# Grouped-query softmax attention: K in 8 KB pieces with two heads on alternate partitions, V in two transfers a pair

## The chip, the cores and the metric

The kernel runs on one core of one Trainium2 chip. The metric is the device time of one execution in microseconds (us). The times of before are the median of three runs; the profile is of one further execution.

## What is computed

There are 16 batches, 32 query heads and 8 key/value heads, so four query heads share one K and one V. Each query head has 16 rows, each K and V has 2048 keys, and the head dimension is 128. All arrays are bf16.

```python
def reference(q, k, v):
    B, Hq, Sq, D = q.shape            # 16, 32, 16, 128
    Hkv = k.shape[1]                  # 8; k, v are (16, 8, 2048, 128)
    k = jnp.repeat(k, Hq // Hkv, axis=1)
    v = jnp.repeat(v, Hq // Hkv, axis=1)
    scores = jnp.einsum("bhqd,bhkd->bhqk", q, k) * D ** -0.5
    p = _softmax(scores, axis=-1)
    return jnp.einsum("bhqk,bhkd->bhqd", p, v)
```

## The kernel before

The 128 combinations of batch and K/V head are worked off in NP = 64 pairs. The 4 x 16 query rows of one K/V head fill 64 rows, so a pair fills the 128 partitions: head g of the pair has rows 64g to 64g+63. K and V of one pair are 1 MB each; a chunk of Q holds the rows of eight pairs (256 KB).

Per pair p the work goes through these steps.

- SyncE (the SP queue) issues every transfer, in a written-out order: K of pair t, then V of pair t-3 (`VLAG`), then the store of pair t-7 (`SLAG`), with a chunk of Q now and then. It waits when a buffer is not free: six K buffers `Kn` (freed by the transposes, L142), eight V buffers `Vb` (freed by the PV matmuls, L152). In `Kn`, a partition holds 16 successive keys (4 KB) of head 0 and 16 of head 1; `Vb` is laid out in the same way.
- VectorE transposes K in 32 x 32 blocks of four bytes, one instruction for each head (`kt`, L254 to L264), into one of three `KT` buffers.
- TensorE multiplies: 32 matmuls of 512 columns into the single `S_ps` (L217). They read `KT` as bf16 with every second element skipped.
- VectorE multiplies the scores by minus the scale, writes them to `Sneg` in f32 and keeps each row's minimum, which is minus the maximum (L277).
- ScalarE writes the exponentials to `P` in bf16, with the sum of each row (L306). It reads `Sneg` in another order than it is stored in, and so sets the order of the keys in `P`.
- TensorE transposes `P` in eight blocks, two bf16 as one f32 (L232), ScalarE copies them to `PT` (L316), TensorE multiplies with V (L243, 32 matmuls), and ScalarE scales the result by the reciprocal of the sum (L326). SyncE stores it (L166).

TensorE and ScalarE follow the lists `pe_prog` and `act_prog`, VectorE the loop at L273. S of pair p+1 is put ahead of the transposes and PV of pair p. The transposes of K for pair p+2 come behind the minimum of pair p. So the loads run some pairs ahead of the arithmetic.

Of the kernel before, what the change touches and what calls it, by code (L numbers as in the profile page):

```python
# [5 lines left out]
ACT = mybir.ActivationFunctionType  # L6
ALU = mybir.AluOpType
BF16 = mybir.dt.bfloat16
# [15 lines left out]
def bass_standalone__gqa_softmax__sampling_kernel(  # L24
# [21 lines left out]
    iota_t = sb("iota_t", [128, 128], I32)  # L46
    ident = sb("ident", [128, 128], BF16)
    ident4 = sb("ident4", [128, 128], F32)
    Kn = [sb(f"Kn{i}", [128, 2, J * 128], BF16) for i in range(NK)]
    Vb = [sb(f"Vb{i}", [128, 2, J, 128], BF16) for i in range(NV)]  # L50

    KT = [sb(f"KT{i}", [128, 2, J * 64], F32) for i in range(NKT)]
    Qn = [sb(f"Qn{i}", [128, 8, 128], BF16) for i in range(NQ)]

    QT = [sb(f"QT{i}", [128, 4, 1024], BF16) for i in range(2)]
# [27 lines left out]

    qf = q.rearrange("b h s d -> (b h s) d")
    of = out.rearrange("b h s d -> (b h s) d")
    kf = k.rearrange("b h s d -> (b h) (s d)").rearrange("g (a x) -> a g x", a=128)
    vf = v.rearrange("b h s d -> (b h) (s d)").rearrange("g (a x) -> a g x", a=128)


    pe_prog, act_prog = [], []
# [35 lines left out]
    with nc.Block() as block:  # L128
# [8 lines left out]
        @block.sync  # L137
        def _(sp):
            def load_k(p):
                s = p % NK  # L140
                if p >= NK:
                    sp.wait_ge(sem_kt, 2 * (p - NK) + 2)  # L142
                if p == 0:
                    for g in range(2):
                        sp.dma_start(Kn[s][:, g, :], kf[:, g, :]).then_inc(sem_k0[g], 16)  # L145
                else:
                    sp.dma_start(Kn[s][:, :, :], kf[:, 2 * p:2 * p + 2, :]).then_inc(sem_k[s], 16)

            def load_v(p):
                s = p % NV  # L150
                if p >= NV:
                    sp.wait_ge(sem_pv, p - NV + 1)  # L152
                dst = Vb[s][:, :, :, :].rearrange("a g j d -> a g (j d)")
                sp.dma_start(dst, vf[:, 2 * p:2 * p + 2, :]).then_inc(sem_v[s], 16)

            def load_q(c):
                s = c % NQ
                if c >= NQ:
                    sp.wait_ge(sem_st, last_q[c - NQ, 3] + 1)
                src = qf[1024 * c:1024 * (c + 1), :].rearrange("(a j) d -> a j d", j=8)  # L160
                sp.dma_start(Qn[s][:, :, :], src).then_inc(sem_q[s], 16)

            def store(p):
                s = p % NO
                sp.wait_ge(sem_nm, p + 1)
                sp.dma_start(of[128 * p:128 * (p + 1), :], Osb[s][:, :]).then_inc(sem_o[s], 16)  # L166

            for t in range(NP + SLAG + 1):
                if t < NP:
                    load_k(t)  # L170
                for c in range(NQC):
                    if t == max(0, 8 * c - QLEAD):
                        load_q(c)
                if 0 <= t - VLAG < NP:
                    load_v(t - VLAG)
                if 0 <= t - SLAG < NP:
                    store(t - SLAG)
            for s in range(NO):
                sp.wait_ge(sem_o[s], 16 * (NP // NO))

        @block.tensor
        def _(pe):
            pe.wait_ge(sem_id, 3)

            def free(u):
                if u >= NSTAGE:
                    pe.wait_ge(sem_ev, u - NSTAGE + 1)

            for op in pe_prog:
                if op[0] == "QT":  # L190
                    _, c, i, u = op
                    if i == 0:
                        pe.wait_ge(sem_q[c % NQ], 16 * (c // NQ + 1))
                    free(u)
                    dst = stage_ap(u).bitcast(BF16)
                    src = Qn[c % NQ][:, :, :].rearrange("p j (b c e) -> p j b e c", b=2, e=2)
                    b, e = divmod(i, 2)
                    for j in range(8):
                        for r in range(4):
                            ins = pe.transpose(dst[32 * r:32 * (r + 1), 128 * j:128 * (j + 1)], src[:, j, b, e, :], ident[:, :])  # L200
                    ins.then_inc(sem_st, 1)
                elif op[0] == "S":
                    _, p = op
                    pe.wait_ge(sem_kt, 2 * p + 2)
                    if p >= 1:
                        pe.wait_ge(sem_max, p)
                    c, i = divmod(p, 8)
                    if i == 0:
                        pe.wait_ge(sem_ev, last_q[c, 3] + 1)
                    kt = KT[p % NKT][:, :, :].bitcast(BF16).rearrange("p g (t b x e) -> p g b e t x", t=J // 2, b=2, e=2)  # L210
                    qt = QT[c % 2]
                    for acc in range(4):
                        b, e = divmod(acc, 2)
                        for r in range(4):
                            rows = slice(32 * r, 32 * (r + 1))
                            for g in range(2):
                                ins = pe.matmul(  # L217
                                    S_ps[64 * g:64 * (g + 1), 512 * r:512 * (r + 1)],
                                    qt[rows, acc, 128 * i + 64 * g:128 * i + 64 * (g + 1)],
                                    kt[rows, g, b, e, :, :],  # L220
                                    start=(acc == 0), stop=(acc == 3),
                                )
                    ins.then_inc(sem_s, 1)
                elif op[0] == "PT":
                    _, p, h, u = op
                    if h == 0:
                        pe.wait_ge(sem_exp, p + 1)
                    free(u)
                    dst = stage_ap(u)
                    for t in range(4):  # L230
                        x = 4 * h + t
                        ins = pe.transpose(dst[:, 128 * t:128 * (t + 1)], P[p % 2][:, 128 * x:128 * (x + 1)], ident4[:, :])  # L232
                    ins.then_inc(sem_st, 1)
                elif op[0] == "PV":
                    _, p = op
                    pe.wait_ge(sem_ev, last_p[p, 1] + 1)
                    pe.wait_ge(sem_v[p % NV], 16 * (p // NV + 1))
                    if p >= 1:
                        pe.wait_ge(sem_nm, p)
                    pt = PT[p % NPT][:, :, :].bitcast(BF16).rearrange("p t (q e) -> p t e q", e=2)  # L240
                    for j in range(J):
                        for g in range(2):
                            ins = pe.matmul(  # L243
                                O_ps[64 * g:64 * (g + 1), 0:128],
                                pt[:, j // 2, j % 2, 64 * g:64 * (g + 1)],
                                Vb[p % NV][:, g, j, :],
                                start=(j == 0), stop=(j == J - 1),
                                skip_group_check=True,
                            )
                    ins.then_inc(sem_pv, 1)  # L250

        @block.vector
        def _(dve):
            def kt(p, g):  # L254
                if p == 0:
                    dve.wait_ge(sem_k0[g], 16)
                else:
                    dve.wait_ge(sem_k[p % NK], 16 * (p // NK + (1 if p % NK else 0)))
                if p >= NKT:
                    dve.wait_ge(sem_s, p - NKT + 1)  # L260
                dve.transpose(  # L261
                    KT[p % NKT][:, g, :].rearrange("p (t b a e) -> p t e b a", t=J // 2, b=2, e=2),
                    Kn[p % NK][:, g, :].bitcast(F32).rearrange("p (t e b c) -> p t e b c", e=2, b=2, c=32),
                ).then_inc(sem_kt, 1)  # L264

            def recip(p):
# [1 line left out]
                dve.reciprocal(rrec[:, p:p + 1], rowsum[:, p:p + 1]).then_inc(sem_rec, 1)  # L268

            for p in range(2):  # L270
                for g in range(2):
                    kt(p, g)
            for p in range(NP):  # L273
                dve.wait_ge(sem_s, p + 1)
                if p >= 2:
                    dve.wait_ge(sem_exp, p - 1)  # L276
                dve.tensor_scalar(  # L277
                    Sneg[p % 2][:, :], S_ps[:, :], -scale, None,
                    op0=ALU.mult, op1=ALU.min, accum_out=nbias[:, p:p + 1],
                ).then_inc(sem_max, 1)  # L280
                if p >= 1:
                    recip(p - 1)
                if p + 2 < NP:
                    for g in range(2):
                        kt(p + 2, g)
            recip(NP - 1)

        @block.scalar
        def _(act):
            for op in act_prog:  # L290
# [9 lines left out]
                elif op[0] == "exp":  # L300
                    _, p = op
                    act.wait_ge(sem_max, p + 1)
                    if p >= 2:
                        act.wait_ge(sem_st, last_p[p - 2, 1] + 1)

                    act.activation(  # L306
                        P[p % 2][:, :].bitcast(BF16).rearrange("p (t r x) -> p t r x", t=8, r=4),
                        Sneg[p % 2][:, :].rearrange("p (r t x) -> p t r x", t=8, r=4), ACT.Exp,
                        bias=nbias[:, p:p + 1], scale=-1.0, accum_out=rowsum[:, p:p + 1],
                    ).then_inc(sem_exp, 1)  # L310
                elif op[0] == "pe":
# [44 lines left out]
```

## Time and profile before

| what | value |
|---|---|
| median of 3 runs (lowest, highest) | 358.48 us (357.37, 358.52) |
| profiled execution | 359.66 us; span of its instructions 357.7 us |
| granted TensorE clock | 0.924 |
| busy share PE, DVE, ACT | 69%, 83%, 70% |
| bytes moved by DMA, mean rate | 139.22 MB, 389 GB/s |
| instructions | 12753 |

The busy shares are of the span. An engine counts as busy while one of its instructions runs. The DMA rows give the mean over the 16 DMA engines of the core. A packet is one piece of a transfer that one DMA engine moves; the increment of a semaphore that ends each engine's part of a transfer is a packet of 4 bytes.

### The profile page before, as it was taken

To read this page: it belongs to the slowest core of one execution; us is meant where nothing else is said; L and a number is where in the kernel's file an instruction comes from. 1 tells how busy PE (TensorE), PEld (TensorE's weight loads), DVE (VectorE), ACT (ScalarE), POOL (GpSimd) and SP (SyncE) were. 2 spreads that over 40 slices of the span, in tenths; PEclk is the share of its full clock that TensorE was granted. 3 is DMA by queue.
4 is the path that set the end of the run, shared out by engine and by line. 5 is a ranking of instruction groups with operands and counts; after the bars stand their busy time and mean duration, and the time that the engine had idled before them with its cause. 6 is when DMAs were issued, how large, how long until landed. Compare 5 with 4: busy or idle time off the path is not lost.

```text
span 357.7 us, 12753 instructions
## 1 busy us (share of the span) xinstructions
PE 248.2 (69%) x5632; PEld 171.7 (48%) x5632; DVE 296.1 (83%) x320; ACT 249.4 (70%) x353; POOL 1.4 (0%) x7
## 2 busy tenths in 40 slices
PE   2587786686776587776677775776766777667675
PEld 2355554454444364454444554454544555444444
DVE  2879979979699839998798699699778889996880
ACT  3469867778478568788676588478676688765674
POOL 1000000000000000000000000000000000000000
PEclk9769989999899969999998899899889899998898
DMA  7999999999999999999999999999999999999930
GB/s 292 414 408 408 410 407 408 411 412 412 410 412 409 410 412 407 412 413 408 409 411 412 411 407 410 411 411 413 409 409 412 401 409 410 410 411 404 377 139 7
DMA packets 45253, 139.22 MB, mean 389 GB/s; under 512 B 11408, under 2 KB 11408, under 8 KB 45200
## 3 DMA queue, kind: packets, MB, share of 16 engines
q1 hardware_dynamic: 45200, 138.42, 97.4%
q8 instruction: 44, 0.72, 0.8%
q14 instruction: 9, 0.07, 0.1%
HBM read 136.31 MB, written 2.10 MB: 387 GB/s over the span
## 4 chain that ended last, share of the span: by engine, by line
PE 51%; issue 26%; ACT 17%; DVE 3%; DMA 1%; SPq 0%; DVEq 0%; ACTq 0%
PE O_ps L243 20%; PE S_ps L217 18%; ACT PT L316 14%; PE ST_ps L232 8%; PE ST_ps L200 5%; DVE KT L261 2%; ACT QT L296 2%; DMA Qn<-in_q_dram 1%; ACT P L306 1%; DVE Sneg L277 1%; SPq L145 0%; ACT O L326 0%; DVE rrec L268 0%; DVEq L276 0%; ACTq L315 0%
## 5 line engine op out<-in xcount | busy, mean ns | idle before, releaser
L277 DVE TENSOR_SCALAR_CACHE_REDUCE Sneg<-S_ps 128x2048 f32<-128x2048 f32 x64 | 146.1, 2283 | 46.1 <-PE S_ps L217 45.7
L261 DVE STREAM_TRANSPOSE KT<-Kn 128x1024 f32<-128x1024 f32 x128 | 150.7, 1216 | 6.9 <-DMA Kn<-in_k_dram 6.9
L306 ACT ACTIVATE P<-Sneg,nbias 128x2048 bf16<-128x2048 f32 x64 | 128.4, 2006 | 24.1 <-DVE Sneg L277 24.1
L243 PE MATMUL O_ps<-Vb,PT 128*64 128x128 bf16 x2048 | 76.3, 230 | 84.3 <-ACT PT L316 55.4
L243 PEld LDWEIGHTS O_ps<-Vb,PT 128*64 128x64 bf16 x2048 | 65.6, 116 | 100.3 <-ACT PT L316 68.0
L316 ACT ACTIVATE PT<-ST_ps 128x512 f32<-128x512 f32 x128 | 70.1, 596 | 38.8 <-PE ST_ps L232 38.8
L217 PE MATMUL S_ps<-KT,QT 32*64 32x512 bf16 x2048 | 82.5, 432 | 6.1 <-DVE Sneg L277 2.5
L232 PE MATMUL ST_ps<-ident,P 128*128 128x128 f32 x512 | 76.3, 296 | 6.5 <-ACT P L306 6.2
L232 PEld LDWEIGHTS ST_ps<-ident,P 128*128 128x128 f32 x512 | 60.4, 151 | 28.7 <-ACT P L306 18.0
L296 ACT ACTIVATE QT<-ST_ps 128x1024 bf16<-128x1024 bf16 x32 | 32.4, 1023 | 36.0 <-PE ST_ps L200 35.8
L217 PEld LDWEIGHTS S_ps<-KT,QT 32*64 32x64 bf16 x2048 | 28.5, 110 | 30.3 <-issue 13.4
L200 PE MATMUL ST_ps<-ident,Qn 128*32 128x128 bf16 x1024 | 22.9, 239 | 10.0 <-DMA Qn<-in_q_dram 6.4
L200 PEld LDWEIGHTS ST_ps<-ident,Qn 128*32 128x32 bf16 x1024 | 17.2, 106 | 23.9 <-issue 23.8
L326 ACT ACTIVATE O<-O_ps,rrec 128x128 bf16<-128x128 f32 x64 | 23.0, 360 | 6.4 <-PE O_ps L243 6.2
L306 ACT ACTIVATION_READ_ACCUMULATOR P<-Sneg,nbias 128x1 f32 x64 | 12.5, 195 | 0.0
L268 DVE RECIPROCAL rrec<-rowsum 128x1 f32<-128x1 f32 x64 | 10.1, 158 | 2.1 <-ACT P L306 2.1
L277 DVE DVE_READ_ACCUMULATOR Sneg<-S_ps 128x1 f32 x64 | 5.3, 82 | 0.0
L296 ACT ACT_TABLE_LOAD x1 | 1.3, 1283 | 0.7 <-PEq L341 0.7
L134 POOL TENSOR_SCALAR ident<-iota_t 128x128 bf16<-128x128 int32 x1 | 0.5, 534 | 0.1
L135 POOL TENSOR_SCALAR ident<-iota_t 128x128 f32<-128x128 int32 x1 | 0.5, 526 | 0.0
L132 POOL IOTA iota_t<- 128x128 int32 x1 | 0.2, 234 | 0.4 <-POOLq L341 0.4
L341 POOL MEMSET const-bfloat16-1.0<- 128x1 bf16 x1 | 0.1, 101 | 0.0
(3 smaller groups left out, 0.3 us busy)
## 6 DMA issues: line engine op xcount, KB each, us to landing
Vb<-in_v_dram SPq DMA_DIRECT2D x64, 1024.0 KB, 16.0
Kn<-in_k_dram SPq DMA_DIRECT2D x63, 1024.0 KB, 15.0
Qn<-in_q_dram SPq DMA_DIRECT2D x8, 256.0 KB, 14.3
out_dram<-O SPq DMA_DIRECT2D x64, 32.0 KB, 13.9
Kn<-in_k_dram SPq DMA_DIRECT2D x2, 512.0 KB, 3.9
```

The costliest lines, as they stand in the source:

```text
L134: gp.tensor_scalar(ident[:, :], iota_t[:, :], 0.0, None, op0=ALU.is_equal).then_inc(sem_id, 1)
L200: ins = pe.transpose(dst[32 * r:32 * (r + 1), 128 * j:128 * (j + 1)], src[:, j, b, e, :], ident[:, :])
L217: ins = pe.matmul(S_ps[64 * g:64 * (g + 1), 512 * r:512 * (r + 1)], qt[rows, acc, 128 * i + 64 * g:128 * i + 64 * (g + 1)], kt[rows, g, b, ...
L232: ins = pe.transpose(dst[:, 128 * t:128 * (t + 1)], P[p % 2][:, 128 * x:128 * (x + 1)], ident4[:, :])
L243: ins = pe.matmul(O_ps[64 * g:64 * (g + 1), 0:128], pt[:, j // 2, j % 2, 64 * g:64 * (g + 1)], Vb[p % NV][:, g, j, :], start=(j == 0), sto ...
L261: dve.transpose(KT[p % NKT][:, g, :].rearrange("p (t b a e) -> p t e b a", t=J // 2, b=2, e=2), Kn[p % NK][:, g, :].bitcast(F32).rearrange ...
L268: dve.reciprocal(rrec[:, p:p + 1], rowsum[:, p:p + 1]).then_inc(sem_rec, 1)
L277: dve.tensor_scalar(Sneg[p % 2][:, :], S_ps[:, :], -scale, None, op0=ALU.mult, op1=ALU.min, accum_out=nbias[:, p:p + 1],).then_inc(sem_max, 1)
L296: act.activation(QT[c % 2][:, i, :].rearrange("p (a j) -> p a j", j=8), stage_ap(u).bitcast(BF16).rearrange("p (j a) -> p a j", j=8), ACT. ...
L306: act.activation(P[p % 2][:, :].bitcast(BF16).rearrange("p (t r x) -> p t r x", t=8, r=4), Sneg[p % 2][:, :].rearrange("p (r t x) -> p t r ...
L316: act.activation(PT[p % NPT][:, 4 * h:4 * (h + 1), :].rearrange("p t q -> p (t q)"), stage_ap(u), ACT.Copy,).then_inc(sem_ev, 1)
L326: act.activation(Osb[p % NO][:, :], O_ps[:, 0:128], ACT.Copy, scale=rrec[:, p:p + 1]).then_inc(sem_nm, 1)
```

## The change

K of a pair is loaded with 32 successive keys (8 KB) of one head in each partition; even partitions belong to head 0 and odd ones to head 1. Each of the two transposes now takes one half of every partition's bytes, 16 keys of both heads, where it took one head before. `KT` gets another layout: the matmul for head g reads pairs of bf16 elements that stand 4 bytes apart, and successive pairs stand 16 bytes apart. The instruction of the minimum writes `Sneg` in a permuted order, in runs of 32 elements, and the exponential reads it in runs of 128 where it read runs of 64. The keys in `PT` are then in an order for which V needs keys of even 4 KB pieces in partitions 0 to 63 and those of odd pieces in 64 to 127. V of a pair is therefore loaded by two transfers of 512 KB to 64 partitions each, and the PV matmuls wait for both. Engine by engine, the sequence of instructions is the same but for SyncE's, which has 64 transfers more (265 instead of 201).

```diff
-    Kn = [sb(f"Kn{i}", [128, 2, J * 128], BF16) for i in range(NK)]
+    Kn = [sb(f"Kn{i}", [128, 2 * J * 128], BF16) for i in range(NK)]
-    KT = [sb(f"KT{i}", [128, 2, J * 64], F32) for i in range(NKT)]
+    KT = [sb(f"KT{i}", [128, 2 * J * 64], F32) for i in range(NKT)]
...
-    kf = k.rearrange("b h s d -> (b h) (s d)").rearrange("g (a x) -> a g x", a=128)
-    vf = v.rearrange("b h s d -> (b h) (s d)").rearrange("g (a x) -> a g x", a=128)
+    kf = k.rearrange("b h s d -> (b h s d)").rearrange("(p g a x) -> p a g x", p=NP, g=2, a=64)
+    vf = v.rearrange("b h s d -> (b h) (s d)").rearrange("g (a h x) -> h a g x", a=64, h=2)
...
                 if p == 0:
-                    for g in range(2):
-                        sp.dma_start(Kn[s][:, g, :], kf[:, g, :]).then_inc(sem_k0[g], 16)
+                    for h in range(2):
+                        x = slice(2048 * h, 2048 * (h + 1))
+                        sp.dma_start(Kn[s][:, x], kf[p, :, :, x]).then_inc(sem_k0[h], 16)
                 else:
-                    sp.dma_start(Kn[s][:, :, :], kf[:, 2 * p:2 * p + 2, :]).then_inc(sem_k[s], 16)
+                    sp.dma_start(Kn[s][:, :], kf[p, :, :, :]).then_inc(sem_k[s], 16)
...
-                sp.dma_start(dst, vf[:, 2 * p:2 * p + 2, :]).then_inc(sem_v[s], 16)
+                for h in range(2):
+                    sp.dma_start(dst[64 * h:64 * (h + 1), :, :], vf[h, :, 2 * p:2 * p + 2, :]).then_inc(sem_v[s], 16)
...
-                    kt = KT[p % NKT][:, :, :].bitcast(BF16).rearrange("p g (t b x e) -> p g b e t x", t=J // 2, b=2, e=2)
+                    kt = KT[p % NKT][:, :].bitcast(BF16).rearrange("p (b m a g x e) -> p g b e m a x", b=2, m=J, a=16, g=2, x=2, e=2)
...
-                    pe.wait_ge(sem_v[p % NV], 16 * (p // NV + 1))
+                    pe.wait_ge(sem_v[p % NV], 32 * (p // NV + 1))
...
                 dve.transpose(
-                    KT[p % NKT][:, g, :].rearrange("p (t b a e) -> p t e b a", t=J // 2, b=2, e=2),
-                    Kn[p % NK][:, g, :].bitcast(F32).rearrange("p (t e b c) -> p t e b c", e=2, b=2, c=32),
+                    KT[p % NKT][:, :].rearrange("p (b h t x e) -> p h t e b x", b=2, h=2, t=J // 2, e=2)[:, h, :, :, :, :],
+                    Kn[p % NK][:, 2048 * h:2048 * (h + 1)].bitcast(F32).rearrange("p (t e b c) -> p t e b c", e=2, b=2, c=32),
...
                 dve.tensor_scalar(
-                    Sneg[p % 2][:, :], S_ps[:, :], -scale, None,
+                    Sneg[p % 2][:, :].rearrange("p (m r x) -> p r m x", r=4, x=32),
+                    S_ps[:, :].rearrange("p (r m x) -> p r m x", r=4, x=32), -scale, None,
...
-                        P[p % 2][:, :].bitcast(BF16).rearrange("p (t r x) -> p t r x", t=8, r=4),
-                        Sneg[p % 2][:, :].rearrange("p (r t x) -> p t r x", t=8, r=4), ACT.Exp,
+                        P[p % 2][:, :].bitcast(BF16).rearrange("p (t h x) -> p t h x", t=8, h=2),
+                        Sneg[p % 2][:, :].rearrange("p (h t x) -> p t h x", t=8, h=2), ACT.Exp,
```

More of the change, by code (lines that the diff above doesn't have):

```diff
@@ L219, in _ @@
                                     qt[rows, acc, 128 * i + 64 * g:128 * i + 64 * (g + 1)],
-                                    kt[rows, g, b, e, :, :],
+                                    kt[rows, g, b, e, :, :, :],
                                     start=(acc == 0), stop=(acc == 3),
@@ L253, in _, with kt @@
         def _(dve):
-            def kt(p, g):
+            def kt(p, h):
                 if p == 0:
-                    dve.wait_ge(sem_k0[g], 16)
+                    dve.wait_ge(sem_k0[h], 16)
                 else:
@@ L270, in _ @@
             for p in range(2):
-                for g in range(2):
-                    kt(p, g)
+                for h in range(2):
+                    kt(p, h)
             for p in range(NP):
@@ L283, in _ @@
                 if p + 2 < NP:
-                    for g in range(2):
-                        kt(p + 2, g)
+                    for h in range(2):
+                        kt(p + 2, h)
             recip(NP - 1)
```

## The prediction

> **What bounds the kernel now.** I first read the page's slices of the span and its DMA queues.
>
> ```profile
> DVE  2879979979699839998798699699778889996880
> DMA  7999999999999999999999999999999999999930
> GB/s 292 414 408 408 410 407 408 411 412 412 410 412 409 410 412 407 412 413 408 409 411 412 411 407 410 411 411 413 409 409 412 401 409 410 410 411 404 377 139 7
> q1 hardware_dynamic: 45200, 138.42, 97.4%
> ```
>
> The compute engines' digits go up and down; the DMA digit is 9 from the second slice to the 38th, and the rate stays at 401 to 414 GB/s up to the 37th. A rate that does not move while its consumers do is a limit of its own. The table by stages says it again: 409 GB/s from 18 to 340 us, at a share over 1, because records of neighbouring packets overlap a little.
>
> ```profile
> 0.00:17.90 17.90, 7.46 (x196) 5.34 (x197) 10.17 (x9) 7.15 (x7) 1.45 (x7) 0.87 0.91 353
> 17.90:340.00 322.10, 230.13 (x5234) 158.54 (x5234) 278.47 (x301) 231.50 (x330) 0.00 (x0) 0.93 1.03 409
> 340.00:357.70 17.70, 10.60 (x212) 7.79 (x206) 7.41 (x12) 10.78 (x16) 0.00 (x0) 0.90 0.20 71
> ```
>
> Then I sorted the trace's records of the packets on that queue by size. The median packet takes 159 ns for 4096 bytes, 84 ns for 2048, 18 ns for 256 and 9 ns for the 4 bytes of a semaphore. That is a straight line: 9 ns for each packet and 0.0366 ns for each byte (27.3 bytes per ns and engine). A pair costs each of the 16 engines 16 packets of K and 16 of V (32 x 159 = 5.09 us), 8 of the store (0.14), three increments (0.03) and an eighth of a Q chunk (0.09): 5.34 us, times 64 = 342 us. All records of the queue add up to 5573.7 us over 16 engines, 348.4 us each; the difference is a small number of long packets. The span is 357.7 us.
>
> Next, the costliest groups and the waits, for how much room the rest has.
>
> ```profile
> L277 DVE TENSOR_SCALAR_CACHE_REDUCE Sneg<-S_ps 128x2048 f32<-128x2048 f32 x64 | 146.1, 2283 | 46.1 <-PE S_ps L217 45.7
> L261 DVE STREAM_TRANSPOSE KT<-Kn 128x1024 f32<-128x1024 f32 x128 | 150.7, 1216 | 6.9 <-DMA Kn<-in_k_dram 6.9
> L306 ACT ACTIVATE P<-Sneg,nbias 128x2048 bf16<-128x2048 f32 x64 | 128.4, 2006 | 24.1 <-DVE Sneg L277 24.1
> L217 PE MATMUL S_ps<-KT,QT 32*64 32x512 bf16 x2048 | 82.5, 432 | 6.1 <-DVE Sneg L277 2.5
> ```
>
> VectorE is the busiest. Where it runs closed up, the timeline has the minimum at 151.04 and again at 155.57 us: 4.53 us a pair, against 5.34 of DMA. So there is 0.8 us a pair of cover over VectorE. The chain that ended last is 51% TensorE and 26% "issue" and names DMA for 1% only; I read it behind the rate, because the arithmetic's loops wait on each other and hide that buffers arrive late. SyncE's waits (next fence) show buffers that are not yet free; its issues, 0.42 us at the start, have a median of 1.2 us (K) and 2.2 us (V) later, so the queue itself is also full.
>
> ```profile
> SPq L154 <- PE O_ps L243: 66.0, 36, 3.9
> SPq L166 <- ACT O L326: 43.0, 36, 5.6
> SPq L147 <- DVE KT L261: 17.1, 11, 4.0
> ```
>
> **K in 8 KB pieces.** For 63 pairs, 16 packets of 4 KB per engine become 8 of 8 KB. By the line an 8 KB packet takes 9 + 300 = 309 ns; the trace has packets of 8192 bytes on the queue that loads instructions (q14), the shortest at 307 to 309 ns. Two old packets take 318, so 8 x 9 = 72 ns a pair are saved: 63 x 0.072 = -4.5 us. The bounds are 0 (the piece is cut at 4 KB again) and -4.5. I take -4.5, since the 8192-byte records are there. Pair 0 keeps two transfers of 4 KB pieces: 0.
>
> **V in two transfers, the issue.** Each of the 64 added transfers brings one increment per engine, 64 x 9 ns = +0.6 us. On SyncE the added issue costs 0.42 us, the smallest of L154; queued behind it are the store and the next K. 64 x 0.42 = 27 us are covered by the 126 us of waits above. Without that cover it would be 27 us at most. I take 0. The PV matmuls wait for the later half, where they waited for the whole; V comes ahead of use by the depth of eight buffers: 0.
>
> **V in two transfers, the transport.** This is the term that decides, and the trace has no row for it: every transfer of before spans 128 partitions. The lower bound is that a packet to one of 64 partitions still takes 159 ns: 0. The upper bound is that a transfer to half of the partitions takes as long as one to all: 16 x 159 = 2.54 us more per pair, 64 x 2.54 = +163 us. Between them lies the case in which the 16 engines, served by half as many doors to the partitions, move their payload back to back on eight: 256 packets over eight at 150 ns (the line's 300 ns for 8 KB, halved) are 4.80 us instead of 2.54, so +2.26 a pair, +144 us. I take this, near the upper end, as a judgement: the rate of the line is the same for loads and stores and for all sizes, which speaks for a fixed width on the way to the partitions rather than for a cost of memory; a fixed width for a part of the partitions is lost when that part is not addressed.
>
> The semaphore records qualify it. The 16 engines' increments for one transfer lie 0.5 us apart at the start of the run and 7 to 9 us late in it, so engines drift. If two engines share a door, they collide while both are in the same half, and while one is in K and the other in a half through the same door; only a lead of about one half transfer (1.27 us) in one direction frees them. Averaged over leads across the 5.1 us of a pair, the overlap that frees is 1.27 x 1.27 / 5.1 = 0.32 us, twice per pair, of 2.54: (2.54 - 0.64) x 0.89 (300 against 2 x 159 = 318, less the gaps; rounded from 2.26 / 2.54) = 1.69 us, or +108 us. The slowest pair of engines sets when a buffer is complete, which is why I keep 144 and not 108.
>
> The Trainium skill has a measured rule against this edit. In "SBUF — State Buffer", under the heading on the DMA port swizzle, 64 partitions from 0 reach only eight of 16 ports and gave 196 GB/s where 128 gave 328; the section on issuing two DMAs for both halves adds that two such transfers at once gained 6% over one. By its 196 GB/s, V of a pair (1.049 MB) would take 5.35 us, +180 us in all as an estimate; no run here shows it yet.
>
> **The arithmetic.** The transposes keep 1024 elements each; their writes already go in steps of 8 bytes and take 1216 ns, so the new steps cost 0. The minimum writes runs of 32 elements: 2283 ns for 2048 contiguous elements is about the transposes' rate per element, which write scattered, so 0; the bound above is one transposed rate (2 x 1216 = 2432), +0.15 us a pair, inside the 0.8. The exponential reads longer runs: 0, no gain on the path. The matmuls of S read two elements of each 16 bytes where they read four: a median of 383 ns now; from no gain (0) to twice (+1.1 us for the group of 32, which takes 1.11 us closed up). I take 0, because the old read already skips every second element. Doubled, it would reach VectorE through S_ps in the 42 pairs whose minimum waits for S, and 1.1 - 0.8 = 0.3 us of it would show: 13 us in the faster case, nothing in the slower one.
>
> **The sum.** Against the profiled execution: 359.66 - 4.5 + 0.6 + 144 = 499.8 us. The median stands 1.2 us below that execution, so 499 us.
>
> **The rivals.**
>
> *Faster: a half transfer keeps the packet time.* Mechanism: the engine, not the partitions, sets the 159 ns. Then only the packet saving counts: 358.48 - 4.5 + 0.6 = 354.6 us, down to 352 if fewer descriptors also spare some of the long packets. For it: each engine keeps 16 packets of V, all 16 engines take part, and the line's 27.3 bytes per ns could be the engine's. Against it: nothing in the trace tells these apart, and the engines' common rate fits a door as well. The point at which the sign turns is a mean packet of V of 159 + 3.9 us / 1024 packets = 163 ns. 0.26; within 0.3% of before if the 8 KB pieces are cut, or the matmuls take some of it back: 0.04.
>
> *Slower, but relieved by drift.* The leads between engines free more than the average above: 365 to 450 us. 0.08.
>
> *Slower twice: K as well.* K's source now has 64 x 2 rows for 128 partitions. If its rows are dealt to the engines in another manner than before, two engines could meet on one door in K too: 128 packets over eight doors at 300 ns are 4.80 instead of 2.47 us, 63 x 2.33 = +147 us, 646 us. Against it: the destination still spans 128 partitions. 0.10.
>
> *The forecast,* V at half rate: 0.52. Its own range is 455 (all of the average relief, and part of the tail hidden) to 525 (the upper bound 359.7 - 3.9 + 163 = 519 and a few long packets).
>
> **How the numbers follow.** Slower by over 0.3% (about the smallest step this measurement tells from none) is 0.52 + 0.08 + 0.10 = 0.70, faster 0.26, within 0.04. The forecast's range alone leaves out 0.48; reaching to the faster case (352) brings in 0.26 + 0.04 + 0.08, and K at half rate stays outside.
>
> **What would show it.** Right: the GB/s digits fall to near 290 (138.4 MB over some 480 us) while the DMA share stays at 9; V's 4 KB packets have a median near 300 ns while K's have 309 for 8 KB; PE waits for V or VectorE for K; VectorE's share falls to about 60%. Wrong: V's packets at 159 ns and a rate over 410. K's 8 KB packets near 600 ns would be the double case; 2.4 us or more at L277, or 500 ns at L217, would be a mis-sized arithmetic term.

## The result and the profile after

The changed kernel takes 592.62 us (median of 4 runs, 589.12 to 597.44), before 358.5 us: a ratio of 1.654, 95% interval [1.641, 1.668]. The sign was forecast; the size lies outside the range given (352 to 525) and 94 us above the forecast of 499. The profiled execution took 597.44 us, its span is 595.6 us.

The slices and the queue of the changed kernel:

```profile
DVE  3745464464465554453636446364563553644542
DMA  8999999999999999999999999999999999999960
GB/s 324 240 236 240 241 239 249 245 245 246 241 240 242 257 254 243 243 232 245 233 236 233 234 237 232 239 242 238 229 237 249 237 236 242 233 230 236 227 155 12
q1 hardware_dynamic: 38160, 138.43, 98.2%
```

The DMA digit is 9 as before, but the rate is about 240 GB/s instead of 410, for the same 138.4 MB. The engines are busy all the time; their packets have become long. The packets are fewer (38160 against 45200): the 8 KB pieces are there. The stage table has the same rate through the run:

```profile
0.00:20.00 20.00, 8.50 (x196) 5.34 (x197) 10.21 (x9) 7.15 (x7) 1.45 (x7) 0.87 0.90 297
200.00:300.00 100.00, 55.42 (x925) 36.09 (x927) 51.09 (x55) 43.45 (x60) 0.00 (x0) 0.74 1.03 243
400.00:500.00 100.00, 60.94 (x1014) 40.17 (x1015) 50.49 (x53) 43.73 (x60) 0.00 (x0) 0.69 1.03 238
```

The groups (instructions, busy time, mean ns of one, idle before and what ended it) and SyncE's waits:

```profile
L283 DVE TENSOR_SCALAR_CACHE_REDUCE Sneg<-S_ps 128x2048 f32<-128x2048 f32 x64 | 146.7, 2292 | 281.7 <-PE S_ps L221 281.7
L265 DVE STREAM_TRANSPOSE KT<-Kn 128x1024 f32<-128x1024 f32 x128 | 150.7, 1216 | 7.5 <-DMA Kn<-in_k_dram 7.5
L313 ACT ACTIVATE P<-Sneg,nbias 128x2048 bf16<-128x2048 f32 x64 | 128.3, 2004 | 16.6 <-DVE Sneg L283 16.2
L221 PE MATMUL S_ps<-KT,QT 32*64 32x512 bf16 x2048 | 129.7, 631 | 3.9 <-DVE Sneg L283 2.5
L247 PE MATMUL O_ps<-Vb,PT 128*64 128x128 bf16 x2048 | 112.1, 294 | 230.7 <-issue 226.4
```
```profile
SPq L170 <- ACT O L333: 55.3, 31, 8.3
SPq L150 <- DVE KT L265: 46.1, 15, 5.9
SPq L158 <- PE O_ps L247: 16.7, 6, 6.0
```

VectorE and ScalarE's own times are those of before. The minimum waits 281.7 us for S, where it waited 46; TensorE in its turn stands 226.4 us before PV with "issue", the name for a wait that the profile ties to nothing. That is the place where V is needed, and V is late: by the times of the increments, PV starts within 0.4 us of V's landing in 61 of 64 pairs, and 2.8 us (median) after `PT` was ready. The matmuls of S take 631 instead of 432 ns (medians 627 and 383). The granted clock is lower too, 0.733 instead of 0.924, but it is not the reason: e3_k_alone has 626 ns at a clock of 0.979. This second effect is hidden here and comes back below.

The trace's records of the packets, sorted by size, carry the rest. This table gives mean (median) ns; "spread" is the median distance between the first and the last engine's increment for one K:

| kernel | K packet | V packet | queue's records per engine | spread |
|---|---|---|---|---|
| before | 162 (159), 4 KB; K and V together | | 348.4 us | 5.6 us |
| changed | 516 (541), 8 KB | 287 (292), 4 KB | 584.7 us | 16.2 us |
| e1_v_halves | 271 (278), 4 KB; K and V together | | 580.5 us | 12.8 us |
| e6_v_quarters | 274 (284), 4 KB; K and V together | | 590.6 us | 11.7 us |
| e3_k_alone | 311 (309), 8 KB | 162 (159), 4 KB | 342.3 us | 5.2 us |
| e10_k_v_near | 359 (318), 8 KB | 281 (301), 4 KB | 498.0 us | 1.5 us |
| e9_k_v_apart | 370 (309), 8 KB | 280 (299), 4 KB | 501.2 us | 0.6 us |

Where K and V both come in 4 KB packets the records do not tell them apart; in the other rows, the 4 KB packets include the 256 of pair 0's K. In e9_k_v_apart, K's mean is far above its median because the queue runs empty before each K: the 16 packets that start a K take 735 ns in the mean, the others 317. In the changed kernel a pair costs an engine 16 x 0.287 = 4.59 us for V (2.54 before) and 8 x 0.516 = 4.13 us for K (2.47 expected).

The records also tell how many V packets were under way on all 16 engines while a K packet of the changed kernel was moved (a mean over the K packet's time, without pair 0's K; 54 packets between and beyond the rows are left out):

| V packets under way | K packets | median, ns |
|---|---|---|
| none (under 0.2) | 358, all in the first 13 us | 309 |
| 1 to 2 | 227 | 379 |
| 2 to 4 | 775 | 549 |
| 4 to 6 | 2307 | 545 |
| 6 to 8 | 1716 | 532 |
| 8 to 10 | 1222 | 541 |
| 10 to 12 | 1157 | 569 |
| 12 to 14 | 248 | 572 |

### The profile page after: what moved, and what is told of

Same layout as the page of the kernel before. It is cut to its first block, busy times and chain, and to the rows that moved or that the text cites. A ratio compares the mean times of both kernels' runs of the same rounds, so it can differ in the third digit from the quotient of the medians.

```text
span 595.6 us, 12817 instructions
## 1 busy us (share of the span) xinstructions
PE 349.4 (59%) x5632; PEld 227.3 (38%) x5632; DVE 297.6 (50%) x320; ACT 255.5 (43%) x353; POOL 1.5 (0%) x7
## 3 DMA queue, kind: packets, MB, share of 16 engines
q1 hardware_dynamic: 38160, 138.43, 98.2%
## 4 chain that ended last, share of the span: by engine, by line
PE 50%; issue 36%; ACT 9%; DMA 3%; SPq 1%; DVE 0%; DVEq 0%; ACTq 0%
PE S_ps L221 20%; PE O_ps L247 19%; ACT PT L323 9%; PE ST_ps L236 8%; PE ST_ps L204 3%; DMA Vb<-in_v_dram 3%; SPq L150 0%; SPq L148 0%; SPq L165 0%; DVE Sneg L283 0%; SPq L158 0%; DVE rrec L272 0%; ACT QT L303 0%; ACT O L333 0%; ACT P L313 0%
## 5 line engine op out<-in xcount | busy, mean ns | idle before, releaser
L283 DVE TENSOR_SCALAR_CACHE_REDUCE Sneg<-S_ps 128x2048 f32<-128x2048 f32 x64 | 146.7, 2292 | 281.7 <-PE S_ps L221 281.7
L247 PE MATMUL O_ps<-Vb,PT 128*64 128x128 bf16 x2048 | 112.1, 294 | 230.7 <-issue 226.4
L247 PEld LDWEIGHTS O_ps<-Vb,PT 128*64 128x64 bf16 x2048 | 99.1, 159 | 246.1 <-issue 243.1
L265 DVE STREAM_TRANSPOSE KT<-Kn 128x1024 f32<-128x1024 f32 x128 | 150.7, 1216 | 7.5 <-DMA Kn<-in_k_dram 7.5
L313 ACT ACTIVATE P<-Sneg,nbias 128x2048 bf16<-128x2048 f32 x64 | 128.3, 2004 | 16.6 <-DVE Sneg L283 16.2
L221 PE MATMUL S_ps<-KT,QT 32*64 32x512 bf16 x2048 | 129.7, 631 | 3.9 <-DVE Sneg L283 2.5
L323 ACT ACTIVATE PT<-ST_ps 128x512 f32<-128x512 f32 x128 | 71.3, 596 | 86.4 <-PE ST_ps L236 86.0
L236 PE MATMUL ST_ps<-ident,P 128*128 128x128 f32 x512 | 89.6, 331 | 1.7 <-ACT P L313 1.7
L236 PEld LDWEIGHTS ST_ps<-ident,P 128*128 128x128 f32 x512 | 72.4, 173 | 36.9 <-issue 32.0
L221 PEld LDWEIGHTS S_ps<-KT,QT 32*64 32x64 bf16 x2048 | 33.7, 138 | 50.8 <-issue 48.3
L204 PEld LDWEIGHTS ST_ps<-ident,Qn 128*32 128x32 bf16 x1024 | 22.0, 127 | 32.0 <-issue 32.0
L204 PE MATMUL ST_ps<-ident,Qn 128*32 128x128 bf16 x1024 | 28.6, 282 | 7.6 <-DMA Qn<-in_q_dram 7.6
```

Source lines behind the costliest of these rows:

```text
L221: ins = pe.matmul(S_ps[64 * g:64 * (g + 1), 512 * r:512 * (r + 1)], qt[rows, acc, 128 * i + 64 * g:128 * i + 64 * (g + 1)], kt[rows, g, b, ...
L247: ins = pe.matmul(O_ps[64 * g:64 * (g + 1), 0:128], pt[:, j // 2, j % 2, 64 * g:64 * (g + 1)], Vb[p % NV][:, g, j, :], start=(j == 0), sto ...
L265: dve.transpose(KT[p % NKT][:, :].rearrange("p (b h t x e) -> p h t e b x", b=2, h=2, t=J // 2, e=2)[:, h, :, :, :, :], Kn[p % NK][:, 2048 ...
L283: dve.tensor_scalar(Sneg[p % 2][:, :].rearrange("p (m r x) -> p r m x", r=4, x=32), S_ps[:, :].rearrange("p (r m x) -> p r m x", r=4, x=32 ...
L313: act.activation(P[p % 2][:, :].bitcast(BF16).rearrange("p (t h x) -> p t h x", t=8, h=2), Sneg[p % 2][:, :].rearrange("p (h t x) -> p t h ...
L323: act.activation(PT[p % NPT][:, 4 * h:4 * (h + 1), :].rearrange("p t q -> p (t q)"), stage_ap(u), ACT.Copy,).then_inc(sem_ev, 1)
```

## The experiments

The theory after the result, D: a transfer to one half of the partitions (0 to 63 or 64 to 127) reaches half of the doors to them, and K is slow only because the engines run apart and meet other engines' halves of V. Its rivals: K, that the new dealing of K's rows is slow by itself; N, that two transfers are slow whatever they reach.

**V alone, and its three controls.** Run e1_v_halves is the kernel before with this edit. The controls e2_v_by_head, e4_v_even_odd and e6_v_quarters have the lines named in the comments in its place. In all four, PV waits for the increments of all of V's transfers.

```diff
-                sp.dma_start(dst, vf[:, 2 * p:2 * p + 2, :]).then_inc(sem_v[s], 16)
+                for h in range(2):
+                    sp.dma_start(dst[64 * h:64 * (h + 1), :, :], vf[64 * h:64 * (h + 1), 2 * p:2 * p + 2, :]).then_inc(sem_v[s], 16)
# e2:  sp.dma_start(dst[:, h, :], vf[:, 2 * p + h, :])
# e4:  sp.dma_start(dst[h::2, :, :], vf[h::2, 2 * p:2 * p + 2, :])
# e6:  for h in range(4):  sp.dma_start(dst[32 * h:32 * (h + 1), :, :], vf[32 * h:32 * (h + 1), 2 * p:2 * p + 2, :])
```

> The kernel before with V of a pair in two transfers, to partitions 0 to 63 and 64 to 127 (natural order); K as before, 4 KB pieces. Theory D (a transfer to half of the partitions reaches half of the doors, and K is slow in the changed kernel only because the engines run apart and meet others' halves of V): K's own form does not matter, so 560 to 610 us, V's packets near 290 ns and K's 4 KB packets well over 159 (240 to 280). Theory K (the new dealing of K's rows, 64 x 2 for 128 partitions, is a second cause): V alone costs what the prediction said, 460 to 520 us, K's packets near 159 to 200. Theory N (two transfers instead of one, whatever they reach): as D.

589.68 us. Its queue and rate:

```profile
GB/s 333 234 245 253 264 257 264 264 252 242 241 240 247 245 242 242 238 238 239 238 245 242 233 243 231 236 238 243 241 227 221 240 250 242 242 246 245 242 208 57
q1 hardware_dynamic: 46224, 138.43, 99.9%
```

V's split alone gives the changed kernel's time, rate and sum of records. K's new form is no cause of the loss. K's old 4 KB packets must be slowed as well: if V's take the 287 ns of the changed kernel here too, the mean of 271 for both leaves about 254 ns for K's (an estimate). That is against theory K.

> The kernel before with V of a pair in two transfers of 512 KB, one for each head, each to all 128 partitions. D and K: only 64 x 9 ns of increments more, 358.5 to 360 us, V's packets at 159 ns. N: near 590 us.

357.76 us, ratio 1.0002 [0.9973, 1.0032]: two transfers, 64 more issues and their increments cost nothing that can be measured. Theory N falls.

> The kernel before with V of a pair in two transfers of 512 KB, the first to the even, the second to the odd partitions: 64 partitions each, but spread over all of them. D: every door is reached by each transfer, so at most part of the loss: 359 us if each engine keeps to its own doors, up to 430 if the dealing of rows makes engines meet now and then. If the number of partitions itself counted, not which ones, the time would be that of the halves, 500 to 600 us.

358.06 us, ratio 1.0001 [0.9976, 1.0027], the 4 KB packets of K and V at a median of 159 ns. So 64 partitions are no loss when every second one is taken. These two transfers read the same pieces of V as the two of the changed kernel (the even and the odd 4 KB pieces); they only write them to other partitions. So the loss lies in where V is written, not in how it is read:

```profile
GB/s 272 413 409 409 409 409 409 412 409 411 411 411 411 411 409 408 412 412 410 409 411 411 409 409 409 412 412 411 410 412 409 402 403 410 410 412 412 385 212 13
```

> The kernel before with V of a pair in four transfers to 32 successive partitions each (natural order). If 32 partitions reach as many doors as 64 (the skill's table): about the time of the halves, 570 to 650 us, V's packets near 300 ns. If the doors are blocks of successive partitions (32 reach a quarter of them): V's packets at 550 to 640 ns and 900 to 1100 us.

591.67 us, the 4 KB packets of K and V together at a median of 284 ns (278 in the halves). Runs of 32 partitions are as bad as runs of 64 and not worse, which is what the Trainium skill's table ("SBUF — State Buffer", the section on the DMA port swizzle) has: 32 and 64 partitions reach the same eight ports. Which partitions a transfer fills decides, not how many.

**K alone.** The changed kernel with V back in one transfer; the order of the keys is mended in the read of the exponential.

```diff
-                        P[p % 2][:, :].bitcast(BF16).rearrange("p (t h x) -> p t h x", t=8, h=2),
-                        Sneg[p % 2][:, :].rearrange("p (h t x) -> p t h x", t=8, h=2), ACT.Exp,
+                        P[p % 2][:, :].bitcast(BF16).rearrange("p (t a h x) -> p t a h x", t=8, h=2, x=2),
+                        Sneg[p % 2][:, :].rearrange("p (h t a x) -> p t a h x", t=8, h=2, x=2), ACT.Exp,
...
```

> The changed kernel with V in one transfer to 128 partitions in the natural order; the exponential reads the two halves of the keys in alternating runs of two elements, so that the order of keys fits. K stays in 8 KB pieces on alternate partitions. D: K's packets at 309 ns, V's at 159, 4 us less than before by the packets: 354.5 us; with the matmuls of S at their 604 ns and an exponential that may slow down on short runs, up to 370. K: its packets stay over 400 ns and the time lies at 420 to 500 us.

356.89 us, ratio 0.9971 [0.9952, 0.999], faster than before by 0.3%. K's packets are at 309 ns, so its new source is not slow.

```profile
L282 DVE TENSOR_SCALAR_CACHE_REDUCE Sneg<-S_ps 128x2048 f32<-128x2048 f32 x64 | 146.7, 2291 | 41.1 <-PE S_ps L220 36.9
L312 ACT ACTIVATE P<-Sneg,nbias 128x2048 bf16<-128x2048 f32 x64 | 137.5, 2148 | 28.1 <-DVE Sneg L282 28.1
L220 PE MATMUL S_ps<-KT,QT 32*64 32x512 bf16 x2048 | 128.5, 625 | 3.9 <-DVE Sneg L282 2.5
```

By the records the last data land 340.9 us after the queue's first packet, in the profile of before 345.0: the 4.0 us that the packets were to save. The median gained 1.0 of them. S takes 2.0 us a pair instead of 1.1 (timeline), and in the last pairs no load is left to wait for, so that a slower S can show there. The span less that time is 13.6 us here, 12.8 before and 10.3 in e2_v_by_head, so this has the right direction, but the scatter of before is as large and it isn't shown.

**V without K.** As e1, with an early return in K's load for p >= NK.

> As e1_v_halves, but K is loaded for the first six pairs only; the later pairs use the K of six pairs earlier that lies in the buffers, so the scores of pairs 6 to 63 are of other keys. What is left on the queue is V, Q and the stores. If V's halves cost what the prediction's term said (4.80 us a pair, two engines to a door) and the rest of the loss is K meeting them: V's packets at a median of 300 to 320 ns, 4.8 to 5.0 us a pair and 330 to 350 us in all. If V's halves cost more than that by themselves (the whole 9.1 us of a pair less K's 2.5): packets near 410 ns, 430 us.

376.28 us: above what was expected, and not a clean time of V, since SyncE now waits for results to store, whose turn is ahead of the next V, and the queue runs dry between:

```profile
SPq L167 <- ACT O L327: 223.2, 63, 7.9
q1 hardware_dynamic: 30448, 77.61, 92.0%
```

The packets answer the question: a median of 304 ns (16384 of the 17920 packets are V's), and 16 x 304 ns = 4.9 us a pair while the queue is full. V's halves cost by themselves what the prediction said, 4.80 us. The rest of the loss comes with K.

**K and V held apart, and held near.** The changed kernel with waits on SyncE ahead of the issues.

```diff
# e9, ahead of K(p), and ahead of V of pair p, with c = p + VLAG
+                    sp.wait_ge(sem_v[(p - 1 - VLAG) % NV], 32 * ((p - 1 - VLAG) // NV + 1))
...
+                    sp.wait_ge(sem_k[c % NK], 16 * (c // NK + (1 if c % NK else 0)))
# e10, ahead of K(p): K(p - 1) has landed; ahead of V(p): V(p - 1) has landed
```

> The changed kernel with K and V never under way together: SyncE waits until K of a pair has landed before it issues the two halves of V, and until both have landed before it issues the next K. If K is slow only because engines that run apart meet V's halves of other engines: K's 8 KB packets at a median of 309 ns (541 in the changed kernel), V's at 300 to 320; the 16 engines move a pair in about 2.5 + 4.9 us, and with two landings of 1.5 to 2 us to wait for in each pair the time is 670 to 740 us, though the packets are faster. If K is slow for another reason (the form of its source, a slower memory): its packets stay at 450 to 600 ns.

818.14 us: the price of the two waits was put too low, for landing takes 5.3 us (K) and 6.3 us (V) from the issue, and the queue is idle for 39% of the span. K's median is 309 ns, as D has it.

> The changed kernel with engines kept near each other: SyncE issues a K only when the K before it has landed, and a V only when the V before it has landed, so that one K and one V are queued and no engine can run further ahead than that. If running apart is what makes K meet V: K's packets between 309 and 541 ns, and the time 500 to 590 us unless the shorter queue runs dry. If the lead does not matter: K's packets at 541 ns or more and 590 us or more.

555.95 us, ratio 1.552 [1.545, 1.560], with waits that only shorten the queue, and faster than the changed kernel:

```profile
GB/s 257 263 253 241 271 246 271 279 251 267 248 237 253 261 253 273 263 252 247 247 262 268 257 267 265 254 274 272 241 272 280 250 255 265 251 272 271 223 148 99
q1 hardware_dynamic: 38160, 138.43, 90.1%
```

The engines stay within 1.5 us of each other (16.2 in the changed kernel), K's packets have a median of 318 ns (541), and the queue's records are 498.0 us per engine (584.7). So 87 us of the loss go with engines that run apart. The waits also keep fewer transfers queued, but the kernel before has a full queue too and loses nothing. In e9_k_v_apart, where no V is under way beside K, K's packets are at 309 ns, and here the 5387 K packets without V beside them have a median of 314 ns, the other 2677 one of 408.

**Versions meant to keep the gain.** Two lay `KT` out in one dense run for each head, so that S reads every second element as before; they differ in whether the transposes (a) or the minimum (b) write scattered.

```diff
-                    kt = KT[p % NKT][:, :].bitcast(BF16).rearrange("p (b m a g x e) -> p g b e m a x", ...)
+                    kt = KT[p % NKT][:, :].bitcast(BF16).rearrange("p (b g n e) -> p g b e n", b=2, g=2, e=2)
# transposes write: a  "p (b g a h k) -> p h k b a g"     b  "p (b g h k a) -> p h k b a g"
# minimum writes:   a  in order                           b  "p (r a k) -> p r k a"
```

> As e3_k_alone, with KT laid out so that the matmuls of S read every second element of one dense run, as before, instead of pairs 16 bytes apart; the transposes pay with writes of 4 bytes scattered at 128 bytes, the minimum writes in order, the exponential reads runs of two at 64 bytes. If the spaced read is what makes S take 2.0 us a pair instead of 1.1: 383 ns a matmul again, and the packets' whole saving shows, 353.5 to 355.5 us. If the scattered writes slow the transposes, VectorE has 0.8 us a pair of room for 2.4 us of transposes: from a third more on, slower than before.

> As e7_k_dense_a, but KT is written in two streams of adjacent 4 byte words (one for each head), and the minimum writes scattered at 128 bytes. If scattered writes cost nothing on VectorE: the same time as e7_k_dense_a, 353.5 to 355.5 us. If they cost in one of the two instructions, the two kernels differ, and the one whose instruction keeps its 1216 or 2292 ns is the faster.

398.76 us (ratio 1.113) and 486.84 us (1.359). In (a), S is back at a median of 383 ns. Neither expected time came: in both VectorE became the bound, at 96% and 97%:

```profile
L264 DVE STREAM_TRANSPOSE KT<-Kn 128x1024 f32<-128x1024 f32 x128 | 316.8, 3177 | 6.3 <-DMA Kn<-in_k_dram 6.3
L264 DVE STREAM_TRANSPOSE KT<-Kn 128x1024 f32<-128x1024 f32 x128 | 246.1, 1994 | 6.1 <-DMA Kn<-in_k_dram 6.1
L282 DVE TENSOR_SCALAR_CACHE_REDUCE Sneg<-S_ps 128x2048 f32<-128x2048 f32 x64 | 232.9, 3639 | 1.3 <-PE S_ps L220 1.3
```

The first line is of (a), where a record also holds time in which its neighbour still runs; two transposes take 5.3 us in its timeline, 2.35 before. The others are of (b): two interleaved streams of 4-byte words cost the transpose 1994 instead of 1216 ns, and steps of 128 bytes cost the minimum 3639 instead of 2283.

The last gives each half of the partitions to one head: K of a pair is one contiguous 1 MB, in 128 rows of 8 KB, and V is one transfer.

```diff
+    kf = k.rearrange("b h s d -> (b h s d)").rearrange("(p a x) -> p a x", p=NP, a=128)
...
+                            for r in range(4):
+                                g, m = divmod(r, 2)   # row group r works for head g
+                                    S_ps[64 * g:64 * (g + 1), 512 * (2 * m + h):512 * (2 * m + h + 1)],
```

> A version meant to keep the packets' saving and to avoid both costs. K in 8 KB pieces with head 0 in partitions 0 to 63 and head 1 in 64 to 127, V in one transfer in natural order; the matmuls of S read every second element of a dense run again, each group of 32 rows works for one head (four row groups with 8 rounds each, where eight pairs of row and column groups shared the work before). If the spaced read is what makes S take 2.0 us and the array's four groups are enough: S at 1.1 to 1.7 us a pair and 353.5 to 356 us. If half of the column groups idle costs S as much as the spaced read: 2.0 us or more, 356 to 360 us.

356.15 us, ratio 0.9944 [0.9911, 0.9977]: the lowest ratio of all, 2.0 us below before. Each matmul is back at a median of 382 ns, but with four pairs of row and column groups in use instead of eight the 32 of them again take 2.0 us (timeline), which was the second case of the expectation. K's packets are at 309 ns and V's at 159.

```profile
GB/s 275 427 411 414 416 413 412 416 415 413 417 417 413 418 413 414 416 413 415 414 416 417 415 412 415 416 414 417 416 413 416 420 415 416 415 413 414 360 137 7
q1 hardware_dynamic: 37136, 138.42, 96.7%
```

## Why the prediction was right in sign and wrong in size

- **The bound** was read rightly: the DMA digit stays at 9 in the changed kernel, and the time follows the packets.
- **K in 8 KB pieces**: right. 309 ns a packet, and the data land 4.0 us earlier in e3_k_alone, against 4.5 in the sum.
- **The issue and the increments**: right (e2_v_by_head). A reason beside them was not: V does not come ahead of use by the depth of eight buffers. Already in the profile of before, PV starts within 0.4 us of V's landing in 42 of 64 pairs.
- **V's transport**: the mechanism and the term held. 4.80 us a pair were predicted; 4.59 was measured in the changed kernel, 64 x (4.59 - 2.54) = 131 us against the 144 of the sum. When all engines are in the halves together, from 14 to 16 us of the queue's time, V's packets have a median of 311 ns, near the 300 that the prediction has for two engines to a door.
- **The step that failed is the paragraph on drift.** It said that engines which run apart relieve the loss, and priced every collision within one fixed pair of engines, so that K and V together could lose 2.26 us a pair at most. The runs show the opposite sign. In the first 12 us of the queue, before V, K's packets take 309 ns; from there on they have V packets of other engines beside them, and take about 550. With leads up to 20 us, K is always in company: 4.13 instead of 2.47 us a pair, 64 x 1.66 = 106 us that the sum lacked. 131 + 106, and 5 for the stores' packets (28 instead of 18 ns, 8 x 64 of them), are 242 us. The sum without V's transport is 359.66 - 4.5 + 0.6 = 355.8 us; with the 242 it is 598, and the profiled execution took 597.44. The queue's records agree: 584.7 - 348.4 = 236 us more per engine, against 242 - 4.5 + 0.6 = 238. Held near, they come to 498.0 us; before's 348.4 with the prediction's terms (-4.5 + 0.6 + 144) are 488.5, so the forecast was nearly that of engines in step.
- **The rival "K as well"** had a time nearer the truth (646), and the sign that would show it, K's packets near 600 ns, nearly came (541). That is luck, for the cause was another: K's source is not slow, and e1_v_halves has K's old form and the same loss. It was left outside the range; a drift with the other sign was not among the cases at all.
- **The matmuls of S**: taken as 0, wrong. With the spaced read a matmul takes 626 against 383 ns (medians, e3_k_alone and before). The loss is hidden behind V here; that it costs a part of the gain in e3_k_alone is likely but not shown.
- **The transposes, the minimum and the exponential**: 1216, 2292 and 2004 ns, right. But the reason given, that scattered writes are free on VectorE, does not hold in general: the minimum lost nothing in runs of 32 elements (2292 against 2283 ns), but took 1.6 times as long in steps of 128 bytes (3639 ns, e8_k_dense_b).

What stays open is why K's packets are slowed as much as they are: which engine writes which partitions is not in the records. A fixed pair of engines for each door, with K kept to its own door, cannot lose more than 2.26 us a pair; 3.7 were lost (2.05 + 1.66). With 2 to 4 V packets under way beside about 12 K packets, such pairs would slow at most 4 of the 12 at a time; but 92% of the 775 K packets in that row of the table took over 400 ns. So either more engines than two share a door, or the engines share something else. No run tells which; doors as such are inferred from the partitions that lost and those that did not.

## What to carry to other kernels

Here a transfer that fills a run of 64 successive partitions moves at about half the rate (4 KB packets at 304 instead of 159 ns without K beside them), and runs of 32 cost the kernel the same. Where engines run apart it also drags down the full-width transfers queued beside it (8 KB packets at 541 instead of 309 ns). Ask which partitions a transfer fills before how many: two transfers by head, or to even and odd partitions, were free (ratios 1.0002 and 1.0001). When a layout needs the halves, see whether a compute engine with room can mend the order instead; here the exponential did it for 0.14 us a pair.

## What the runs showed that was not expected

- The 16 DMA engines drift apart by themselves: 0.5 us between their first and last increment at the start of the kernel before, 8 to 9 us late in it, where the rate is still 401 to 414 GB/s; 20 us in the changed kernel.
- A matmul whose moving operand takes two bf16 of each 16 bytes needs 626 ns for 512 columns (e3_k_alone, granted clock 0.979), against 383 when it takes every second element of a dense run (before, 0.924).
- VectorE's transpose of 1024 elements takes 1216 ns with writes in steps of 8 bytes, 1.6 times as long in two interleaved streams (1994 ns), and in steps of 128 bytes about 2.65 us (5.3 for two). The minimum takes 1.6 times as long in steps of 128 bytes. ScalarE's read in runs of two elements takes 2148 against 2006 ns.
